# A long convolution beside block attention on one core: filter turned by TensorE, loads on one queue, a split last product, and a new instruction order

## The chip, the cores and the metric

The kernel runs on one NeuronCore of a Trainium2 chip. The core has five engines that run side by side and meet through semaphores: TensorE (PE, matmuls; its weight loads are listed as PEld), VectorE (DVE), ScalarE (ACT), GpSimd (POOL) and SyncE (SP, which here only issues DMAs). A DMA can be issued from SP, ACT or POOL; it takes its place in that engine's instruction stream. The metric is the device time of one execution in microseconds (us). The profile covers one execution; its span runs from the first to the last instruction, and the time lies a little above it.

## The reference

Two independent computations share the kernel, and their outputs stand side by side in the columns of the result.

```python
# A: gated long convolution, S = 2048 positions, D = 640 channels
k_shift = sum(k_pad[:, t:t+S, :] * shift_k[:, ks-1-t] for t in range(4))
kv = k_shift * v
y  = irfft(rfft(kv, 2*S) * rfft(ssm_k, 2*S))[:S] + kv * ssm_D
a  = q * y
# B: 32 heads of 20, four segments of 512 positions
for s in range(4):
    p     = softmax(q_s @ k_s^T * scale + causal_mask)
    a_mem = phi(q_s) @ M / (phi(q_s) @ z + 1e-6)
    o_s   = g * a_mem + (1 - g) * (p @ v_s)
    M, z  = M + phi(k_s)^T @ v_s, z + sum(phi(k_s))
b = concat(o) @ wo
out = concatenate([a, b], axis=-1)
```

## The kernel before, in words

**Part A** runs over five blocks `dp` of 128 channels (`a_chunks`). The transform is done as matmuls with the tables `Wf` (forward) and `Wi` (inverse) for each of four phases `c` (position = 4p + c), joined by butterflies on DVE. For each block: `load_kv` fetches `vt` (v) and `kr` (k, transposed by DMA); `kshift` makes the short filter on PE with the diagonal weights `skd`, and DVE multiplies into `vt`; `fwd("X", c)` transforms it, ACT casting each PSUM bank into `F`; `bfly("X")` is the DVE butterfly into `Xh`. The long filter takes the same way: `load_sk` fetches 128 rows of `ssm_k`, DVE copies them so that the phases stand together (`kT<-kT`, a COPY of 128x2048), a DMA transposes the copy into `kT`, and `fwd("K", c)` and `bfly("K")` give `Kh`. Then DVE multiplies the spectra into `S` (`pointwise`, `ybfly`), PE inverts (`inverse`), DVE multiplies with q into `outa`, and POOL stores it.

**Part B** runs over eight units `u`, that is four segments `s` and two halves of 16 heads. `b_proj_chunks` loads x transposed (`xT`), projects it with `wqkv` in four pieces of 128 positions (three groups of five matmuls each into the two `b` banks; ACT casts them to `KQ` and `Va`; DMAs transpose `KQ` into `KT` and `QT`), and finds a bound for each row of logits (`bound`: `kam`, `A`, `tq`, `bT`), which four small DMAs put into row 20 of each 32-row band of `QT`. `b_attn_chunks` spreads `KT` into `KZ` (POOL DMAs) and does four groups `attn(g)`: logits on PE into the three `st` banks, exp on ACT into `ET`, causal mask on DVE, product with `Va` and the memory into the one `o` bank, and division and sum on DVE into `o_s`. After the second half of a segment four DMAs transpose `o_s` into `oT` (`outt`), and `outproj` multiplies with `wo`: two groups of 320 columns for each of four pieces, cast by ACT into `outb`, stored by POOL.

**Order.** No order is written by hand. `Recorder` records all operations, prices each (`price`), and `plan` runs a list scheduler forwards and backwards with the priorities of the table `BIAS` and the earliest times of the table `HOLD`; `emit` then issues them in that order, so each engine's stream is fixed before the run. Every operation carries a key such as `('A', dp, stage)`. All emitted instructions therefore carry the line of `emit` (L435 before, L438 after). PSUM has eight banks: 3 `st`, 2 `a` (part A), 2 `b`, 1 `o`.

DMAs on the hardware queues (SP and ACT) get one of eight semaphores, `DMAHW0` to `DMAHW7`, in turn; a DMA waits at its issue until the one eight before it has landed. The listings of order show these waits.

Of the kernel before, what the change touches and what calls it, by code (L numbers as in the profile page):

```python
# [15 lines left out]
ALU = mybir.AluOpType  # L16
# [64 lines left out]
class Op:  # L81
    __slots__ = ("eng", "calls", "key", "bank", "new", "dur", "lat", "dma", "pred", "succ", "tail", "idx", "late")
# [11 lines left out]
class Recorder:  # L94


    def __init__(self, tc):
        self.tc, self.real = tc, tc.nc
        self.nc = ProxyNC(self)
        self.ops, self.key = [], ("const",)  # L100
        self.live, self.masks = {}, {}
        self.slots, self.home, self.turn, self.rows = {}, {}, {}, {}
# [32 lines left out]
    def add(self, eng, method, args, kw):  # L135
# [3 lines left out]
        e = QUEUES[eng]  # L139
# [6 lines left out]
        if method == "matmul" and bank.last is not None and bank.last.eng == "PE":  # L146
            op = bank.last
        if op is None:
# [3 lines left out]
            op.pred, op.succ, op.dur, op.lat = {}, [], 0.0, 0.0  # L152
            self.ops.append(op)
            if bank is not None:
                bank.left += 1
                bank.ops.append(op)
# [22 lines left out]
    def price(self, op, method, out, ins):  # L179
# [5 lines left out]
        elif method in ("dma_start", "dma_start_transpose"):  # L185
            src = ins[0]
            size = int(np.prod(list(out.shape))) * mybir.dt.size(out.dtype)
            if method == "dma_start_transpose":
                packets, per = size / 256, 23.5
                dram = src.space == bass.MemoryType.DRAM  # L190
                op.dur = 650.0 + 560.0 * size / 131072 + (600.0 if dram else 0.0)
# [6 lines left out]
        elif op.eng == "ACT":  # L198
            op.dur, op.lat = n / 1.152 + 33, 210.0
        elif op.eng == "DVE":  # L200
            fast = all(two(a) and a.space != bass.MemoryType.PSUM and int(a.ap[-1][0]) == 1 for a in [out] + ins)
            if method == "tensor_tensor":
                op.dur = n / (1.92 if fast else 0.96) + 60
            elif method == "tensor_reduce":
                op.dur = int(np.prod(list(ins[0].shape)[1:])) / 0.96 + 60
            elif method == "reciprocal":
                op.dur = 67 + 6.1 * n
            else:
                op.dur = n / (3.84 if fast else 1.2) + 60
# [65 lines left out]
    def backward(self, prio):  # L275
# [19 lines left out]
        while times:  # L295
# [3 lines left out]
            for e in free:  # L299
# [34 lines left out]
                for p in o.late:  # L334
                    j = p.idx
                    r = end + (0 if p.dma is None and p.eng == e and e != "PE" else self.lag(p))
# [8 lines left out]
    def forward(self, prio, held):  # L345
# [19 lines left out]
        while times:  # L365
# [3 lines left out]
            for e in free:  # L369
# [31 lines left out]
                else:  # L401
                    fin, near = end + o.lat, end + (0 if e != "PE" else o.lat)
# [41 lines left out]
class K3:  # L444
    def __init__(self, ctx, tc, A_q, A_k, A_v, A_shift_k, A_ssm_k, A_ssm_D, B_x, B_wq, B_wk, B_wv, B_wo, B_beta, out):
# [30 lines left out]
        def wload(engs, half):  # L476
# [67 lines left out]
    def a_chunks(self, dp):  # L544
# [6 lines left out]
        def load_sk():  # L551
            sk = self.ring("kT", [128, 4, 4, 128], n=2)[:].rearrange("p a b d -> p (a b d)")
            nc.sync.dma_start(out=sk, in_=self.ssm_k[dsl, :])
            skp = self.ring("kT", None, n=2)
            nc.vector.tensor_copy(out=skp[:], in_=sk.rearrange("d (b p c) -> d c b p", b=4, c=4))
            Drow = st["Drow"] = self.ring("Drow", [1, 128])
            nc.gpsimd.dma_start(out=Drow[:], in_=self.ssm_D[None, dsl])
            kT = st["kT"] = self.ring("kT", None, n=2)
# [114 lines left out]
        Kc = [(load_sk, 0.1)] + [(fwd("K", c), 2.0) for c in range(4)] + [(bfly("K"), 5.5)]  # L673
# [3 lines left out]
    def b_proj_chunks(self, u):  # L677
# [32 lines left out]
        def bound():  # L710
# [37 lines left out]
        return ch  # L748

    def b_attn_chunks(self, u):  # L750
# [13 lines left out]
        def attn(g):  # L764
            def f():
# [21 lines left out]
                for qh in range(2):  # L787
# [19 lines left out]
                    else:  # L807
                        o2 = self.ring("o2", [128, 2, 8, DH], n=2)
                        V.tensor_tensor(out=o2[:], in0=pov[:, :, :, 0:DH], in1=rr[:, :, :, None].to_broadcast([128, 2, 8, DH]), op=ALU.mult)
                        V.tensor_tensor(out=odst, in0=o2[:, 0].rearrange("p (q h) e -> p q h e", h=4), in1=o2[:, 1].rearrange("p (q h) e -> p q h e", h=4), op=ALU.add)  # L810
# [18 lines left out]

        ch = [(attn(g), 7.0) for g in range(4)]  # L830
        pre = [(spread(g), 0.1) for g in range(2)]
        tail = [(outt, 0.1)] + [(outproj(t), 1.5) for t in range(4)] if half == 1 else []
# [130 lines left out]
```

## Time and profile before

| | us |
|---|---|
| three runs | 355.88, 362.82, 357.06; median 357.06 |
| the profiled execution's own time | 355.69 |
| its span | 353.7 |
| PE busy / DVE busy / ACT busy / POOL busy | 302.4 / 305.7 / 278.0 / 80.5 |
| mean granted TensorE clock | 0.97 of full speed |

Three engines are each busy for more than three quarters of the span. The shares alone do not say which one holds the time, so the span is best cut into a start, a long middle and an end, with each engine's busy time in each piece. In the profile's rows, "idle before" names what ended an engine's idle time; in the chain of waits each row is a start, a duration, and what held the chain then. A row such as `SPq ... DMA_TRANSPOSE` gives the time in which SP was issuing, not the time in which the data moved. Names are `out<-in` with buffer numbers left out.

### The profile page before, as it was taken

How to read it: one execution, taken by the hardware profiler on the slowest of the kernel's cores; microseconds unless marked ns; L12 is line 12 of the kernel's file. 1: busy time of each engine (PE TensorE's matmuls, PEld its weight loads, DVE VectorE, ACT ScalarE, POOL GpSimd, SP SyncE). 2: the span in 40 equal slices, each digit the busy share in tenths (PEclk: the TensorE clock that was granted, in tenths of full speed). 3: DMA queues.
4: the chain of work that ended last, by engine and by line, in shares of the span. 5: the costliest groups of instructions: out<-in, count | busy, mean ns of one | idle time of the engine just before them, and what ended most of it. 6: DMA issues, size and time to landing. Idle time of an engine off the chain costs nothing.

```text
span 353.7 us, 9016 instructions
## 1 busy us (share of the span) xinstructions
PE 302.4 (86%) x3462; PEld 217.8 (62%) x3466; DVE 305.7 (86%) x539; ACT 278.0 (79%) x633; POOL 80.5 (23%) x127
## 2 busy tenths in 40 slices
PE   0179699899997699799999999999989998888584
PEld 0157477567785477577766776777766675555363
DVE  2016999999999999899999999999998998999960
ACT  1046648999979989889989999989986998899502
POOL 9402410214112110312024005230060040312023
PEclk9999999999999899899999999999998999999869
DMA  9976766969557335705598358537430564302043
GB/s 262 212 141 165 159 141 98 256 117 199 112 114 186 73 62 113 134 17 74 150 130 202 74 126 142 117 68 105 100 92 26 91 105 70 92 30 69 0 101 110
DMA packets 110267, 40.97 MB, mean 116 GB/s; under 512 B 102624, under 2 KB 107264, under 8 KB 109968
## 3 DMA queue, kind: packets, MB, share of 16 engines
q1 hardware_dynamic: 100768, 29.50, 43.7%
q0 software_dynamic: 5088, 8.09, 8.9%
q10 hardware_dynamic: 4368, 2.81, 2.8%
q8 instruction: 27, 0.44, 0.5%
q14 instruction: 16, 0.13, 0.1%
HBM read 13.36 MB, written 5.24 MB: 53 GB/s over the span
## 4 chain that ended last, share of the span: by engine, by line
PE 33%; DVE 28%; issue 14%; DMA 8%; ACT 6%; SPq 6%; POOL 3%; POOLq 0%; ACTq 0%; DVEq 0%
PE b L435 13%; PE a L435 9%; PE st L435 7%; DVE S L435 7%; SPq L435 6%; PE o L435 4%; DVE ET L435 4%; DMA KT<-KQ 3%; DVE Xh L435 3%; ACT ET L435 3%; DVE kam L435 3%; DMA kr<-in_A_k_dram 2%; POOL out_dram L435 2%; DMA oT<-o_s 1%; DVE o L435 1%
## 5 line engine op out<-in xcount | busy, mean ns | idle before, releaser
L435 ACT ACTIVATE ET<-st 128x512 bf16<-128x512 f32 (+1 forms) x384 | 185.2, 575 | 11.6 <-PE st L435 10.5
L435 PE MATMUL st<-QT,KZ 128*128 128x384 bf16 (+2 forms) x508 | 105.1, 301 | 6.3 <-ACT ET L435 3.9
L435 PE MATMUL b<-wqkv,xT 128*128 128x320 bf16 x480 | 79.3, 303 | 18.8 <-DMA xT<-in_B_x_dram 16.0
L435 PEld LDWEIGHTS <-xT 128*128 128x128 bf16 x480 | 45.8, 99 | 37.6 <-DMA xT<-in_B_x_dram 16.0
L435 POOL DMA_DIRECT2D KZ<-KT x64 | 40.0, 629 | 123.0 <-PE st L435 91.1
L435 PEld LDWEIGHTS <-KZ 128*128 128x128 bf16 x512 | 45.6, 98 | 28.0 <-issue 12.2
L435 PEld LDWEIGHTS <-ET 128*128 128x128 bf16 x1280 | 41.8, 96 | 24.1 <-DVE ET L435 11.5
L435 PE MATMUL o<-Va,ET 128*128 128x21 bf16 x1280 | 44.2, 173 | 12.0 <-DVE ET L435 5.9
L435 ACT CAST F<-a 128x512 bf16<-128x512 f32 x80 | 48.4, 624 | 5.5 <-PE a L435 5.0
L435 ACT CAST KQ<-b 128x320 bf16<-128x320 f32 x64 | 30.0, 472 | 19.4 <-PE b L435 17.4
L435 DVE TENSOR_TENSOR ET<-ET,cmask 128x1024 bf16<-128x1024 bf16 x64 | 43.0, 682 | 0.4 <-ACT ET L435 0.4
L435 PEld LDWEIGHTS <-Wf 128*128 128x128 bf16 x320 | 30.3, 99 | 15.8 <-issue 8.8
L435 DVE TENSOR_TENSOR S<-S 128x2048 bf16<-128x2048 bf16 (+1 forms) x40 | 37.2, 950 | 0.2
L435 POOL DMA_DIRECT2D out_dram<-outa x20 | 15.4, 769 | 71.5 <-DVE outa L435 52.7
L435 PE MATMUL b<-wo,oT 128*128 128x320 bf16 x160 | 28.0, 314 | 0.6 <-DMA oT<-o_s 0.6
L435 PE MATMUL a<-kT,Wf 128*128 128x256 bf16 x160 | 24.3, 274 | 2.9 <-DVE outa L435 1.9
L435 ACT CAST outb<-b 128x320 bf16<-128x320 f32 x32 | 14.9, 480 | 14.1 <-PE b L435 14.1
L435 DVE TENSOR_TENSOR o<-o,rr 128x320 bf16<-128x320 f32 x48 | 23.6, 491 | 1.6
L435 PE MATMUL a<-vt,Wf 128*128 128x256 bf16 x160 | 23.3, 280 | 1.4 <-ACT F L435 0.7
L435 PE MATMUL a<-S,Wi 128*128 128x256 bf16 x160 | 22.2, 286 | 1.5 <-DVE S L435 1.5
L435 DVE TENSOR_TENSOR S<-Xh,Kh 128x4096 bf16<-128x4096 bf16 x10 | 22.8, 2284 | 0.1
L435 PE MATMUL a<-skd,kr 128*128 128x128 bf16 x320 | 22.0, 224 | 0.4 <-DMA kr<-in_A_k_dram 0.2
(61 smaller groups left out, 385.0 us busy)
## 6 DMA issues: line engine op xcount, KB each, us to landing
KZ<-KT POOLq DMA_DIRECT2D x64, 42.0 KB, 2.9
kT<-in_A_ssm_k_dram SPq DMA_DIRECT2D x5, 512.0 KB
qd<-in_A_q_dram SPq DMA_DIRECT2D x20, 128.0 KB
out_dram<-outa POOLq DMA_DIRECT2D x20, 128.0 KB, 2.8
out_dram<-outb POOLq DMA_DIRECT2D x16, 160.0 KB, 2.1
vt<-in_A_v_dram SPq DMA_DIRECT2D x16, 128.0 KB
Wf<-c_wf ACTq DMA_DIRECT2D x1, 1024.0 KB
Wi<-c_wi SPq DMA_DIRECT2D x1, 1024.0 KB
```

The costliest lines, as they stand in the source:

```text
L435: f(*[fix(a) for a in args], **{k: fix(v) for k, v in kw.items()})
```

## The change

1. **Long filter.** The DVE copy and the DMA transpose of `load_sk` are gone. A new stage `turn(c)`, four for each block, multiplies four strided slices of the loaded rows with the identity on PE (128x128 each, into one `a` bank), and ACT casts the bank into `kT`. The loaded rows now have a buffer `sk` of their own, one, and `kT` is one buffer instead of two.
2. **Loads.** `Wf`, the first half of the projection weights (three loads) and the four `vt` loads of block 0 are issued on SP instead of ACT. `skc`, `ident`, `kr` and `xT` were on SP already.
3. **Bound rows.** The four DMAs from `bT` into `QT` become one with a partition step of 32.
4. **Last product.** For the last segment `o_s` is kept as features 0 to 511 and features 512 to 639. Four DMAs transpose the first part, one the second. The product with `wo` is made 512 columns wide in four banks (three `st`, one `b`) over the first four feature blocks, and the last feature block is added later, in a separate piece; the remaining 128 columns go to one `b` bank. DVE and ACT share the casts, and SP and ACT issue the stores. Head group 3 of the last unit lies in the second part alone.
5. **Planner.** Prices change (a stall of 115 ns after a reciprocal, ACT on SBUF data dearer, DVE copies from PSUM cheaper), and `BIAS` and `HOLD` are replaced whole, so the order changes everywhere.

```diff
         def load_sk():
-            sk = self.ring("kT", [128, 4, 4, 128], n=2)[:].rearrange("p a b d -> p (a b d)")
-            nc.sync.dma_start(out=sk, in_=self.ssm_k[dsl, :])
-            skp = self.ring("kT", None, n=2)
-            nc.vector.tensor_copy(out=skp[:], in_=sk.rearrange("d (b p c) -> d c b p", b=4, c=4))
+            sk = st["sk"] = self.ring("sk", [128, S])
+            nc.sync.dma_start(out=sk[:], in_=self.ssm_k[dsl, :])
+            st["kT"] = self.ring("kT", [128, 4, 4, 128])
...
-            nc.sync.dma_start_transpose(out=kT[:].rearrange("p c b d -> p (c b) d"), in_=skp[:].rearrange("d c b p -> d (c b p)"))
+        def turn(c):
+            def f():
+                ps = self.bank("a")
+                phase = st["sk"][:].rearrange("d (b p c) -> d c b p", b=4, c=4)
+                for b in range(4):
+                    nc.tensor.matmul(ps[:, 128 * b:128 * b + 128], lhsT=phase[:, c, b, :], rhs=ident[:], start=True, stop=True)
+                nc.scalar.copy(out=st["kT"][:, c], in_=ps[:].rearrange("p (b d) -> p b d", d=128))
+            return f
...
-            "Wf": lambda: nc.scalar.dma_start(out=self.Wf[:], in_=self.real.inline_tensor(Wf_np, name="c_wf").ap()),
+            "Wf": lambda: nc.sync.dma_start(out=self.Wf[:], in_=self.real.inline_tensor(Wf_np, name="c_wf").ap()),
-            "w0": wload((nc.scalar,) * 3, 0), "w1": wload((nc.sync,) * 3, 1),
+            "w0": wload((nc.sync,) * 3, 0), "w1": wload((nc.sync,) * 3, 1),
-                (nc.scalar if dp == 0 else nc.sync).dma_start(out=vt[:, b], in_=self.v[512 * b:512 * b + 512, dsl].rearrange("(p c) d -> p c d", c=4))
+                nc.sync.dma_start(out=vt[:, b], in_=self.v[512 * b:512 * b + 512, dsl].rearrange("(p c) d -> p c d", c=4))
...
-            for hl in range(4):
-                r = 32 * hl + DH
-                nc.sync.dma_start(out=QT[r:r + 1, :, :], in_=bT[4 * hl:4 * hl + 4, :])
+            nc.sync.dma_start(out=QT[DH:128:32, :, :], in_=bT[:])
...
+        def out_last():
+            oT = self.ring("oT", None)
+            low, high = self.o_parts(s)
+            for tci in range(4):
+                nc.sync.dma_start_transpose(out=oT[:, 0:4, 128 * tci:128 * tci + 128], in_=low[:, tci, :])
+            nc.sync.dma_start_transpose(out=oT[:, 4, :].rearrange("p (t k) -> p t k", t=4), in_=high)
+            wide = [self.bank(k) for k in ("st", "st", "st", "b")]
+            edge = self.bank("b")
+            for ccs in (range(4), (4,)):
+                for tci in range(4):
+                    self.rec.cut = ccs[0] == 4
...
+            fin = self.ring("ET", None, n=2)[:, :, 0:640]
+            for tci in range(4):
+                (nc.scalar.copy if tci % 2 else V.tensor_copy)(out=fin[:, tci, 0:512], in_=wide[tci][:])
...
+                (nc.scalar if tci % 2 else nc.sync).dma_start(out=self.out[L * s + 128 * tci:L * s + 128 * tci + 128, D:2 * D], in_=fin[:, tci, :])
...
 BIAS = {
-    ('A', 0, 0): 5055, ('A', 0, 1): 3361, ('A', 0, 10): 288761, ('A', 0, 11): 15357, ('A', 0, 12): 174774, ('A', 0, 13): 17992, ('A', 0, 14): -17162,
...
+    ('A', 0, 0): 89953, ('A', 0, 1): 438151, ('A', 0, 10): 1950, ('A', 0, 11): 160004, ('A', 0, 12): -11423, ('A', 0, 13): 619533, ('A', 0, 14): 147551,
```

Three places show how the order moved. The first is SP at the start of the program. Before, with the waits in brackets:

```order
L435 DMA kT_99<-in_A_ssm_k_dram 128x2048
L435 DMA_TRANSPOSE xT_113<-in_B_x_dram 128x5x512
L435 DMA skc<-in_A_shift_k_dram 128x5x4
L435 DMA ident<-c_ident 128x128
L435 DMA_TRANSPOSE kT_99<-kT_100 128x16x128 [waits DMAHW1_49,DMAHW0_49,DVE_49]
L435 DMA_TRANSPOSE kr_105<-in_A_k_dram 128x512
```

SP in the changed kernel at the same place, without the waits; `sk_99` is what was loaded into `kT_99`:

```order
L438 DMA Wf<-c_wf 128x4096
L438 DMA ident<-c_ident 128x128
L438 DMA sk_99<-in_A_ssm_k_dram 128x2048
L438 DMA skc<-in_A_shift_k_dram 128x5x4
L438 DMA_TRANSPOSE xT_113<-in_B_x_dram 128x5x512
L438 DMA wqkv<-in_B_wk_dram 128x5x320
L438 DMA wqkv<-in_B_wq_dram 128x5x320
L438 DMA wqkv<-in_B_wv_dram 128x5x320
L438 DMA_TRANSPOSE kr_105<-in_A_k_dram 128x512 x3
L438 DMA vt_104<-in_A_v_dram 128x4x128
L438 DMA_TRANSPOSE kr_105<-in_A_k_dram 128x512
L438 DMA vt_104<-in_A_v_dram 128x4x128 x3
```

The tables and the filter now stand ahead of `xT`, and one queue holds every large load in one row.

The second place is ACT at the start, before, where it issues loads between its casts (`KQ`, `Va` and `xm` belong to the projection):

```order
L435 DMA Wf<-c_wf 128x4096
L435 DMA vt_104<-in_A_v_dram 128x4x128 [waits DMAHW2_49]
L435 ACT_TABLE_LOAD
L435 CAST KQ_80<-b_66 128x16x20 [waits PE_49]
L435 ACTIVATE xm_115<-KQ_80 128x320 [waits Activation_49]
L435 DMA vt_104<-in_A_v_dram 128x4x128 [waits DMAHW7_49]
L435 CAST KQ_80<-b_67 128x16x20 [waits PE_49]
L435 DMA bt<-in_B_beta_dram 128x32 [waits DMAHW0_49]
L435 CAST Va_83<-b_66 128x16x20 [waits PE_49]
```

ACT at the start of the changed kernel:

```order
L438 ACT_TABLE_LOAD
L438 CAST kT_100<-a_64 128x512 [waits PE_49]
L438 CAST kT_100<-a_65 128x512 [waits PE_49]
L438 CAST kT_100<-a_64 128x512 [waits PE_49]
L438 CAST F_102<-a_65 128x512 [waits PE_49]
L438 CAST F_102<-a_64 128x512 [waits PE_49]
L438 CAST F_102<-a_65 128x512 [waits PE_49]
L438 CAST F_102<-a_64 128x512 [waits PE_49]
L438 CAST kT_100<-a_65 128x512 [waits PE_49]
L438 CAST F_102<-a_64 128x512 [waits PE_49]
L438 CAST F_102<-a_65 128x512 [waits PE_49]
L438 CAST KQ_80<-b_66 128x16x20 [waits PE_49]
```

The filter's casts now come first and the projection's after them; only `bt` is still loaded from ACT here.

The third place is DVE at the end of the program, before (`o_128` and `o_129` are the two buffers `o2`, `outa` the gated output of part A):

```order
L435 TENSOR_TENSOR outa_112<-a_64,qd_108 128x512
L435 RECIPROCAL rr_124<-o_68 128x16
L435 TENSOR_TENSOR o_129<-o_68,rr_124 128x320
L435 TENSOR_TENSOR o_s_120<-o_129 128x2x80
L435 TENSOR_TENSOR outa_111<-a_65,qd_108 128x512
L435 TENSOR_TENSOR outa_112<-a_64,qd_108 128x512
```

DVE at the end of the changed kernel:

```order
L438 TENSOR_TENSOR outa_112<-a_64,qd_108 128x512
L438 TENSOR_TENSOR o_128<-o_68,rr_123 128x320
L438 TENSOR_TENSOR o_s_120<-o_128 128x2x80
L438 RECIPROCAL rr_124<-o_68 128x16
L438 TENSOR_TENSOR o_129<-o_68,rr_124 128x320
L438 TENSOR_TENSOR o_s_120<-o_129 128x2x80
L438 CAST ET_121<-b_66 128x128 x2
L438 CAST ET_121<-st_62 128x512
L438 CAST ET_121<-st_61 128x512
```

All of part A's outputs now stand ahead of the last `o_s`, and behind it are only the casts of the last product. On PE, 8 of the 20 wide matmuls now stand ahead of the last group's second product with `Va` and 8 right behind it; the 20 of 128 columns and the other 4 wide ones come last.

More of the change, by code (lines that the diff above doesn't have):

```diff
@@ L81 @@
 class Op:
-    __slots__ = ("eng", "calls", "key", "bank", "new", "dur", "lat", "dma", "pred", "succ", "tail", "idx", "late")
+    __slots__ = ("eng", "calls", "key", "bank", "new", "dur", "lat", "dma", "pred", "succ", "tail", "idx", "late", "stall")
 class Bank:
@@ L100, in __init__ @@
         self.ops, self.key = [], ("const",)
-        self.live, self.masks = {}, {}
+        self.live, self.masks, self.cut = {}, {}, False
         self.slots, self.home, self.turn, self.rows = {}, {}, {}, {}
@@ L145, in add @@
         op = None
-        if method == "matmul" and bank.last is not None and bank.last.eng == "PE":
+        if method == "matmul" and bank.last is not None and bank.last.eng == "PE" and not self.cut:
             op = bank.last
+        self.cut = False
         if op is None:
@@ L151, in add @@
             op.new = bank is not None and bank.last is None
-            op.pred, op.succ, op.dur, op.lat = {}, [], 0.0, 0.0
+            op.pred, op.succ, op.dur, op.lat, op.stall = {}, [], 0.0, 0.0, 0
             self.ops.append(op)
             if bank is not None:
+                if not op.new:
+                    op.pred[bank.ops[0].idx] = bank.ops[0]
                 bank.left += 1
@@ L189, in price @@
                 packets, per = size / 256, 23.5
-                dram = src.space == bass.MemoryType.DRAM
-                op.dur = 650.0 + 560.0 * size / 131072 + (600.0 if dram else 0.0)
+                op.dur = 650.0 + 570.0 * size / 131072
             else:
@@ L198, in price @@
         elif op.eng == "ACT":
-            op.dur, op.lat = n / 1.152 + 33, 210.0
+            op.dur, op.lat = n / 1.152 + (33 if ins[0].space == bass.MemoryType.PSUM or n > 1000 else 95), 210.0
         elif op.eng == "DVE":
+            op.stall = 115 if method == "reciprocal" else 0
             fast = all(two(a) and a.space != bass.MemoryType.PSUM and int(a.ap[-1][0]) == 1 for a in [out] + ins)
@@ L208, in price @@
             else:
-                op.dur = n / (3.84 if fast else 1.2) + 60
+                op.dur = n / (3.84 if fast else 1.9) + 60
             op.lat = 150.0
@@ L335, in backward @@
                     j = p.idx
-                    r = end + (0 if p.dma is None and p.eng == e and e != "PE" else self.lag(p))
+                    r = end + (p.stall if p.dma is None and p.eng == e and e != "PE" else self.lag(p))
                     ready[j] = max(ready[j], r)
@@ L401, in forward @@
                 else:
-                    fin, near = end + o.lat, end + (0 if e != "PE" else o.lat)
+                    fin, near = end + o.lat, end + (o.stall if e != "PE" else o.lat)
                 done_at[i] = fin
@@ L672, in a_chunks @@
         X = [(load_kv, 0.1)] + [(kshift(a), 1.5) for a in range(4)] + [(fwd("X", c), 2.0) for c in range(4)] + [(bfly("X"), 7.0)]
-        Kc = [(load_sk, 0.1)] + [(fwd("K", c), 2.0) for c in range(4)] + [(bfly("K"), 5.5)]
+        Kc = [(load_sk, 0.1)] + [(turn(c), 1.0) for c in range(4)] + [(fwd("K", c), 2.0) for c in range(4)] + [(bfly("K"), 5.5)]
         Dl = [(load_q, 0.1), (pointwise(0), 4.6), (pointwise(1), 5.0), (ybfly, 7.6)] + [(inverse(c), 1.7) for c in range(4)]
@@ L748, in b_proj_chunks, with o_parts, o_pieces @@
         return ch
+    def o_parts(self, s):
+        o = self.o_s[s][:].rearrange("p t h d -> p (t h d)")
+        return o[:, 0:2048].rearrange("p (t f) -> p t f", t=4), o[:, 2048:2560].rearrange("p (t f) -> p t f", t=4)
+    def o_pieces(self, s, f0, q0):
+        if s < NS - 1:
+            return [(self.o_s[s][:].rearrange("p t h d -> p t (h d)")[:, q0:q0 + 2, f0:f0 + 80], 0, 80)]
+        low, high = self.o_parts(s)
+        cut = min(max(512 - f0, 0), 80)
+        return ([(low[:, q0:q0 + 2, f0:f0 + cut], 0, cut)] if cut else []) + ([(high[:, q0:q0 + 2, f0 + cut - 512:f0 + 80 - 512], cut, 80)] if cut < 80 else [])
     def b_attn_chunks(self, u):
@@ L809, in f @@
                         V.tensor_tensor(out=o2[:], in0=pov[:, :, :, 0:DH], in1=rr[:, :, :, None].to_broadcast([128, 2, 8, DH]), op=ALU.mult)
-                        V.tensor_tensor(out=odst, in0=o2[:, 0].rearrange("p (q h) e -> p q h e", h=4), in1=o2[:, 1].rearrange("p (q h) e -> p q h e", h=4), op=ALU.add)
+                        loc, mem = (o2[:, x].rearrange("p (q h) e -> p q (h e)", h=4) for x in range(2))
+                        for dst, a, b in self.o_pieces(s, h0 * DH, 2 * qh):
+                            V.tensor_tensor(out=dst, in0=loc[:, :, a:b], in1=mem[:, :, a:b], op=ALU.add)
             return f
@@ L828, in outproj @@
             return f
+        def out_last():
+            oT = self.ring("oT", None)
+            low, high = self.o_parts(s)
+            for tci in range(4):
[6 more added lines that the diff above has]
+                    self.rec.cut = ccs[0] == 4
+                    for cc in ccs:
+                        nc.tensor.matmul(wide[tci][:], lhsT=oT[:, cc, 128 * tci:128 * tci + 128], rhs=self.wo[:, cc, 0:512], start=(cc == 0), stop=(cc == 4))
+            for tci in range(4):
+                for cc in range(5):
+                    nc.tensor.matmul(edge[:, 128 * tci:128 * tci + 128], lhsT=oT[:, cc, 128 * tci:128 * tci + 128], rhs=self.wo[:, cc, 512:640], start=(cc == 0), stop=(cc == 4))
+            fin = self.ring("ET", None, n=2)[:, :, 0:640]
+            for tci in range(4):
+                (nc.scalar.copy if tci % 2 else V.tensor_copy)(out=fin[:, tci, 0:512], in_=wide[tci][:])
+                (V.tensor_copy if tci % 2 else nc.scalar.copy)(out=fin[:, tci, 512:640], in_=edge[:, 128 * tci:128 * tci + 128])
+                (nc.scalar if tci % 2 else nc.sync).dma_start(out=self.out[L * s + 128 * tci:L * s + 128 * tci + 128, D:2 * D], in_=fin[:, tci, :])
         ch = [(attn(g), 7.0) for g in range(4)]
         pre = [(spread(g), 0.1) for g in range(2)]
-        tail = [(outt, 0.1)] + [(outproj(t), 1.5) for t in range(4)] if half == 1 else []
+        tail = [] if half == 0 else [(out_last, 0.1)] if s == NS - 1 else [(outt, 0.1)] + [(outproj(t), 1.5) for t in range(4)]
         return pre, ch, tail
@@ L837 @@
 BIAS = {
[34 rows of a table removed]
-    ('beta',): -57426, ('const',): 401682, ('load', 'Wf'): -285064, ('load', 'Wi'): -16407, ('load', 'w0'): 90126, ('load', 'w1'): -10388,
-    ('load', 'wo'): -34008,
[38 rows of a table added]
 }
 HOLD = {
[9 rows of a table removed]
[8 rows of a table added]
 }
```

1 line of the change is left out of this document (removed), and 87 rows, old and new, of tables (BIAS, HOLD).

## The prediction

> **What bounds the kernel now.** I read the busy times by stage first, then the chain of waits at the start, then the end. The first view's columns are the stretch, its length, busy time (and count) of PE, PEld, DVE, ACT and POOL, granted clock, DMA share and GB/s. I cut at three DVE events: its first long run (30.58), the first butterfly of X (43.79), and the end of the last `o_s` (341.47 + 0.24 = 341.71).
>
> ```profile
> 0.00:30.58 30.58, 12.29 (x84) 8.13 (x85) 4.82 (x11) 9.35 (x20) 13.97 (x20) 1.00 0.91 203
> 30.58:43.79 13.21, 10.05 (x110) 7.99 (x107) 12.96 (x21) 7.34 (x16) 4.09 (x7) 1.00 0.64 149
> 43.79:341.71 297.92, 272.70 (x3221) 196.56 (x3226) 286.57 (x506) 257.94 (x590) 58.77 (x95) 0.97 0.53 105
> 341.71:353.70 11.99, 7.40 (x52) 5.14 (x50) 1.39 (x3) 3.41 (x8) 3.71 (x6) 0.93 0.42 116
> ...
> 240.00:260.00 20.00, 19.89 (x265) 15.10 (x263) 19.79 (x35) 19.03 (x46) 2.15 (x4) 1.00 0.52 95
> ...
> 30.58 1.23 DVE L435 TENSOR_TENSOR Kh<-F 128x2048 bf16<-128x2048 bf16 x1 [0.15 <-ACT F L435]
> ...
> 43.79 1.22 DVE L435 TENSOR_TENSOR Xh<-F 128x2048 bf16<-128x2048 bf16 x1
> ...
> 341.47 0.24 DVE L435 TENSOR_TENSOR o_s<-o 128x160 bf16<-128x160 bf16 x1
> ```
>
> From 30.58 to 341.71 DVE idles 0.25 + 11.35 us in 311: it carries the kernel there. In the third stage PE idles 25.2 and ACT 40.0. DVE's other idle time is 25.8 us at the start and 10.6 at the end. So span = X butterfly's start + DVE's work from there to the last `o_s` + its idle + tail.
>
> The start: the chain of waits (start, duration, holder) and who waited for `xT`:
>
> ```profile
> 1.21 7.91 SPq L435
> ...
> 18.01 4.15 DMA kr<-in_A_k_dram
> 22.16 0.02 issue
> 22.18 0.56 ACTq L435
> 22.74 0.04 issue
> 22.78 0.43 ACT KQ L435
> ...
> 24.77 0.45 PE a L435 x4
> ...
> PE b L435 <- DMA xT<-in_B_x_dram: 16.0, 1, 16.0
> ```
>
> PE does nothing until `xT` lands at 16.0; its issue takes 7.91 us while four large loads from ACT share the DMA engines. Later a `vt` load on ACT waits for a `kr` transfer until 22.18, and the casts queue behind it.
>
> **The change: the start.** What PE needs first is now `Wf`, `ident` and `sk`.
>
> ```profile
> 2.00:4.00 2.00, 0.00 (x0) 0.00 (x0) 0.00 (x0) 0.00 (x0) 2.00 (x1) 1.00 0.90 296
> ...
> kT<-in_A_ssm_k_dram SPq DMA_DIRECT2D x5, 512.0 KB
> ...
> Wf<-c_wf ACTq DMA_DIRECT2D x1, 1024.0 KB
> ...
> L435 SPq DMA_TRANSPOSE xT<-in_B_x_dram x4: 2899/4466/7912, 1.2 to 216.3; - x4
> ...
> 16.70 5.17 SPq L435 DMA_TRANSPOSE kr<-in_A_k_dram  x4
> ...
> 59.38 1.73 SPq L435 DMA_DIRECT2D Wi<-c_wi  x1
> ...
> 24.14 0.55 ACTq L435 DMA_DIRECT2D vt<-in_A_v_dram  x1
> ...
> L435 ACT CAST F<-a 128x512 bf16<-128x512 f32 x80 | 48.4, 624 | 5.5 <-PE a L435 5.0
> ...
> L435 ACT ACTIVATE xm<-KQ 128x320 bf16<-128x320 bf16 x24 | 12.1, 505 | 1.9 <-DVE PK L435 0.9 <-DVE Mbd L435 0.7
> ...
> 29.44 0.18 DVE L435 TENSOR_SCALAR omginv<-ep 128x32 f32<-128x32 f32 x1 [7.27 <-ACT ep L435]
> ```
>
> 1.5 MB at the 296 GB/s of 2:4 are 5 us after 2.0: the turns start near 7. In its new order ACT then makes 4 `kT` and 8 `F` casts at 0.6 (7.2 us), six projection casts at the chain's 0.43 (2.6), two `xm` and one load, some 0.5 each (1.5): 11.3 us, so the last `F` comes at 18.5, provided `xT` is there when its first cast is due, near 13. Behind the 1.5 MB, with its median issue of 4.47, `xT` should land at about 12. So DVE's long run starts at 18.5 instead of 30.58. Up to the X butterfly it has its 12.96 us, less the 1.22 of the copy (below), plus the 1.1 of `beta` work that it had done from 29.44 to 30.58: 31.4, if it never waits. It also needs `vt`. SP's issues are `Wf` 1.7 (as `Wi`), `xT` 2.9 to 7.9, `kr` 5.2, ten more at 0.55 and 0.8 of gaps: the last `vt` is issued by 17 to 22, against 24.69. After it come the short filter, four forward phases and `kam`, which I let cost DVE 2 us of waits: X butterfly at 33.5 (31.4 to 37), a gain of 10.3. The stall of ACT's loads moves to SP; behind SP's loads stand only loads and the first `KT` and `QT`, whose casts are not made before 14 to 16.
>
> A rule speaks against this. The Trainium skill, Perfetto Trace Analysis, DMA Optimizations, advises balancing DMAs over the engines that can issue them when issuing is the bottleneck. By it, with `xT` at its longest, the last `vt` comes 3 us earlier instead of about 6 and the sum is some 3 us longer; the trace has no start from one queue to decide it, but it shows ACT's casts held by a load.
>
> **The middle.** `kT` alone in the second and third stage (PE, DVE, clock, DMA share, GB/s), a run of 32 matmuls of 128x128, the `o_s` additions (min/median/max ns), and two rows on the bound:
>
> ```profile
> 30.58:43.79 13.21, 0.00 (x0) 1.22 (x1) 1.00 0.64 149
> 43.79:341.71 297.92, 19.70 (x128) 3.94 (x3) 0.97 0.53 105
> ...
> 30.05 1.95 PE a L435 x32
> ...
> L435 DVE TENSOR_TENSOR o_s<-o x48: 178/233/244, 140.9 to 341.5; 128x160 bf16<-128x160 bf16 x48
> ...
> 45.88 2.07 SPq L435 DMA_DIRECT2D QT<-bT  x3
> ...
> PE st L435 <- DMA QT<-bT: 1.2, 1, 1.2
> ```
>
> DVE: 286.57, less three copies (3.94), plus the two `outa` that stood behind the last `o_s` (the fourth stage's 1.39), plus two extra `o_s` pieces (0.4): 284.4. The copies' removal is worth its full price, since DVE is the bound.
>
> PE: 80 turn matmuls at 1.95 / 32 = 0.061, 60 of them in the middle: 3.7. Their weights are read with a step of four elements, which no row shows; bounds are 0.061 and the 0.45 / 4 = 0.11 of the chain's transform matmuls of double width, and I take 0.061, the row of the same size. The Trainium skill, VectorE: DVE Perf Modes, The three transpose paths, gives TensorE 390 ns for one 128x128; by that the 60 would be 23.4 us instead of 3.7 (an estimate), and PE would have more work than DVE. The run of 32 at 0.061 decides for the small price.
>
> ACT: 20 casts at 0.624, 15 in the middle: 9.4 on 257.94. It still idles 30 us, so I cost them at nothing; the cover is DVE's queue of work. If ACT's order delayed exps, PE's products and DVE's masks would be late next.
>
> SP: five transposes and 24 small DMAs fewer. The bound row comes up to three issues of 0.69 sooner, but PE waited for it once, for 1.2 us: between 0 and 1.2 gained, or a little lost if one DMA with 16 rows lands later than four small ones; I take 0. The single `sk` buffer makes the next filter's load wait for the turns, with `KT` and `QT` transposes behind it on SP; the turns run well ahead of those casts in the order, so 0, at worst a few us of the idle below.
>
> DVE's idle, 11.35, I set to 13: PE and ACT are fuller. The row 240:260 has all three above 19 of 20 us with DVE idle 0.21, 3 us over the whole middle; 25, PE's own idle, is the other end.
>
> **The tail.** From the last `o_s` to the end was 11.99.
>
> ```profile
> 140.67 3.13 DMA KT<-KQ
> ...
> 288.75 5.04 DMA oT<-o_s
> ...
> 32.00 0.68 PE b L435 x5
> ...
> 349.92 0.55 POOL L435 DMA_DIRECT2D out_dram<-outb  x1 [0.86 <-ACT outb L435]
> ```
>
> Now: one transpose, 3.1 to 5.0 from issue to user (3.9); 20 matmuls of 128 at 0.061 and 4 of 512 at 0.68 / 5 x 512 / 320 = 0.22 (2.1); casts after the last matmul 0.7; a second store's issue 0.6; store to end 3.8 (353.7 - 349.92), plus hand-overs 0.4: 11.5 (10.5 to 13). The wide product's head start saves 3.5 us of PE at a place where four 320-wide pairs already ran behind transposes, so little is won.
>
> **Sum.** 33.5 + 284.4 + 13 + 11.5 = 342.4 of span, plus 355.69 - 353.7 = 2.0: 344.4 us. That is against the profiled execution's own 355.69 (-3.2%); the median of the runs shown, 357.06, is 1.4 above that.
>
> **Rivals.**
> - *PE becomes the bound.* PE's middle is 272.70 + 3.7 + two inverse groups 2.1 + 16 wide matmuls 3.5 = 282. If it keeps its 25.2 idle, the middle is 307.2 and the time 354.2. For it: PE's 94% of 297. Against: the row 240:260, PE 19.89 of 20. This rival also holds the case that turns do not pipeline.
> - *The start brings nothing but the copy.* If one queue delivers `xT` and `vt` no sooner, the X butterfly comes at 43.79 - 1.22 = 42.6 and the time is 353.5. For it: 0.91 DMA share before 30.58. Against: 12 us in which PE could turn and transform, and ACT freed of loads.
> - *Slower: the clock.* If a fuller PE is granted less, PE binds.
>
> ```profile
> 146.00:148.00 2.00, 0.14 (x6) 0.14 (x6) 1.97 (x4) 2.00 (x4) 1.91 (x4) 1.00 1.27 225
> 148.00:150.00 2.00, 2.00 (x43) 2.00 (x41) 1.90 (x4) 1.30 (x3) 0.78 (x1) 0.62 0.89 146
> ...
> 320.00:340.00 20.00, 14.20 (x195) 9.18 (x195) 18.95 (x37) 11.49 (x28) 2.79 (x4) 0.82 0.16 38
> ```
>
> At 0.82 throughout the middle, 282 x 0.97 / 0.82 = 333.6 and the time is 380.6. Slower by 2% (364.2) begins at a middle of 317.2, a mean clock of 0.86. Against: the clock fell after PE had idled (0.14 of 2 us), and was 1.00 at 19.89 of 20.
>
> **Chances and range.** Forecast 0.70, PE 0.13, start 0.11, clock 0.06. Two per cent, 349.9 to 364.2, is about what a measurement of this kernel tells from no change (its three runs span 1.9%). The first two rivals end within 2%; milder forms of them, some 0.04, lie below 349.9: faster 0.74, same 0.20, slower 0.06. The forecast's own range is 338 (butterfly at 31.4, idle 9, tail 11) to 350 (idle 17, butterfly at 35); up to 354 it takes in most of both rivals.
>
> **What would show it.** Right: `Kh<-F` at 17 to 20 and the first `Xh<-F` at 31 to 37; DVE busy 284 to 285 from there to the last `o_s`, idle 9 to 17; kT casts on ACT at 0.6 with turn matmuls at 0.06; a tail of 10.5 to 13. Wrong: the butterfly later than 40, DVE idle over 20 with PE never idle, or a mean clock below 0.9.

## The result and the profile after

The changed kernel takes 339.53 us (median of four runs, 338.22 to 343.19), the kernel before, run beside it, 358.79 (355.88 to 362.82): a ratio of 0.951 (95% interval 0.938 to 0.963). Times are medians of all runs of a kernel, while ratios compare means without its slow runs (here without the 362.82), so a ratio isn't the quotient of two medians. The profiled execution took 339.53 us, with a span of 337.3. The forecast was 344.4, with a range of 338 to 354.

The same four stages as in the prediction, after, cut at the first `Kh<-F`, the first `Xh<-F` and the end of the last `o_s` (columns: stretch, length, busy time and count of PE, PEld, DVE, ACT, POOL, granted clock, DMA share, GB/s):

```profile
0.00:19.47 19.47, 11.27 (x76) 7.92 (x77) 1.83 (x6) 10.37 (x19) 11.13 (x17) 1.00 0.86 225
19.47:35.50 16.03, 13.20 (x140) 10.67 (x139) 13.23 (x26) 9.62 (x22) 5.48 (x11) 1.00 0.81 171
35.50:327.78 292.28, 275.59 (x3304) 201.69 (x3303) 278.14 (x507) 262.21 (x604) 60.76 (x97) 0.98 0.53 104
327.78:337.30 9.52, 3.19 (x28) 1.82 (x28) 1.78 (x5) 1.51 (x4) 0.00 (x0) 0.99 0.27 83
```

The span lost 16.4 us: 8.3 before X's butterfly, 5.6 in the middle, 2.5 at the end. DVE idles 2.8 us in the second stage and 14.1 in the third. The chain that ended last lies on PE for 60% of the span and on DVE for 9% (before: PE 33%, DVE 28%); the experiments say how far that may be believed:

```profile
PE 60%; ACT 15%; DMA 12%; DVE 9%; issue 4%; SPq 0%; DVEq 0%; ACTq 0%
```

DVE's rows of the timeline after (start, duration, idle before and what ended it) show what came ahead of X's butterfly:

```profile
19.47 1.23 DVE L438 TENSOR_TENSOR Kh<-F 128x2048 bf16<-128x2048 bf16 x1 [0.19 <-ACT F L438]
...
31.69 2.29 DVE L438 TENSOR_REDUCE kam<-KT 128x4 f32<-128x2048 bf16 x1 [1.81 <-DMA KT<-KQ]
...
34.76 0.82 DVE L438 TENSOR_SCALAR tq<-QT 128x2048 int16<-128x2048 int16 x1 [0.52 <-DMA QT<-KQ]
35.50 1.20 DVE L438 TENSOR_TENSOR Xh<-F 128x2048 bf16<-128x2048 bf16 x1
```

Of the 2.8 us of waits, 2.3 are for the transposes of `KT` and `QT`. And the end, after, on all engines:

```profile
327.54 0.24 DVE L438 TENSOR_TENSOR o_s<-o 128x160 bf16<-128x160 bf16 x1
...
330.31 1.07 PE L438 MATMUL b<-wo,oT 128*128 128x128 bf16 x16 [1.11 <-DMA oT<-o_s]
...
331.64 0.59 PE L438 MATMUL st<-wo,oT 128*128 128x512 bf16 x2
...
333.05 0.60 ACT L438 CAST ET<-b 128x512 bf16<-128x512 f32 x1
333.20 0.84 ACTq L438 DMA_DIRECT2D out_dram<-ET  x2
```

From the end of the last `o_s` (327.78) it is 2.5 us to the products of the last transpose, 1.9 to the end of the matmuls (332.23), 1.4 to the last cast's end (333.65), and 3.65 to the end: 9.5.

### The profile page after: what moved, and what is told of

Its sections match the earlier page's. It is cut to its first block, busy times and chain, and to the rows that moved or that the text cites. A ratio compares the mean times of both kernels' runs of the same rounds, so it can differ in the third digit from the quotient of the medians.

```text
span 337.3 us, 9126 instructions
## 1 busy us (share of the span) xinstructions
PE 303.2 (90%) x3546; PEld 222.1 (66%) x3546; DVE 295.0 (87%) x540; ACT 283.7 (84%) x649; POOL 77.4 (23%) x123
## 4 chain that ended last, share of the span: by engine, by line
PE 60%; ACT 15%; DMA 12%; DVE 9%; issue 4%; SPq 0%; DVEq 0%; ACTq 0%
PE b L438 20%; PE a L438 17%; PE st L438 15%; ACT ET L438 10%; PE o L438 7%; DMA QT<-KQ 6%; DMA kr<-in_A_k_dram 2%; ACT F L438 2%; DMA sk<-in_A_ssm_k_dram 2%; DVE S L438 2%; DVE tq L438 2%; DMA oT<-o_s 1%; DVE ET L438 1%; DVE o L438 1%; ACT KQ L438 1%
## 5 line engine op out<-in xcount | busy, mean ns | idle before, releaser
L438 ACT ACTIVATE ET<-st 128x512 bf16<-128x512 f32 (+1 forms) x384 | 193.4, 642 | 6.8 <-PE st L438 6.1
L438 PE MATMUL st<-QT,KZ 128*128 128x512 bf16 (+3 forms) x512 | 109.4, 303 | 6.1 <-ACT ET L438 5.2
L438 ACT CAST F<-a 128x512 bf16<-128x512 f32 x80 | 51.7, 674 | 2.8 <-PE a L438 2.7
L438 ACT CAST KQ<-b 128x320 bf16<-128x320 f32 x64 | 33.7, 526 | 6.9 <-PE b L438 4.0
L438 PE MATMUL a<-kT,Wf 128*128 128x256 bf16 x160 | 26.0, 289 | 0.7 <-ACT F L438 0.6
L438 PE MATMUL b<-wo,oT 128*128 128x320 bf16 (+2 forms) x145 | 23.2, 291 | 1.1 <-DMA oT<-o_s 1.1
L438 PE MATMUL a<-skd,kr 128*128 128x128 bf16 x320 | 21.1, 219 | 1.3 <-DMA kr<-in_A_k_dram 1.1
L438 DVE TENSOR_REDUCE kam<-KT 128x4 f32<-128x2048 bf16 x8 | 18.2, 2275 | 4.0 <-DMA KT<-KQ 4.0
L438 PEld LDWEIGHTS <-kr 128*128 128x128 bf16 x320 | 19.3, 98 | 3.1 <-issue 1.7
```

The costliest lines, as they stand in the source:

```text
L438: f(*[fix(a) for a in args], **{k: fix(v) for k, v in kw.items()})
```

## Experiments

The runs keep the order of the kernel that they alter, except where the edit moves something: it is made after planning. Ratios are to the kernel before, run beside them. The third stage ("middle") of each profiled execution, cut as above:

| | time, us | ratio (95%) | middle | DVE busy | DVE idle | PE busy |
|---|---|---|---|---|---|---|
| before | 358.79 | 1 | 297.92 | 286.57 | 11.35 | 272.70 |
| after | 339.53 | 0.951 (0.938 to 0.963) | 292.28 | 278.14 | 14.14 | 275.59 |
| after_again | 342.32 | 0.953 (0.946 to 0.961) | 295.90 | 278.49 | 17.41 | 277.68 |
| pair | 346.30 | 0.964 (0.954 to 0.974) | 301.67 | 286.48 | 15.19 | 281.44 |
| more | 344.39 | 0.960 (0.951 to 0.968) | 298.16 | 275.78 | 22.38 | 278.52 |
| split (of before) | 358.34 | 0.996 (0.990 to 1.001) | 296.45 | 281.42 | 15.03 | 269.62 |
| dve_more | 358.57 | 1.004 (0.998 to 1.010) | 311.22 | 300.10 | 11.12 | 278.94 |
| act_more | 343.95 | 0.964 (0.956 to 0.972) | 296.37 | 278.48 | 17.89 | 274.76 |
| pe_more | 343.10 | 0.961 (0.954 to 0.969) | 293.97 | 278.46 | 15.51 | 278.79 |
| old_tail | 346.91 | 0.971 (0.962 to 0.980) | 292.79 | 277.15 | 15.64 | 273.44 |
| act_loads | 340.22 | 0.947 (0.942 to 0.952) | 295.31 | 278.05 | 17.26 | 274.90 |
| dma_turn | 347.16 | 0.967 (0.962 to 0.973) | 295.84 | 282.65 | 13.19 | 273.22 |
| rows4 | 344.76 | 0.961 (0.955 to 0.966) | 295.84 | 278.02 | 17.82 | 273.72 |
| conv_split | 341.99 | 0.953 (0.949 to 0.958) | 297.71 | 278.91 | 18.80 | 275.96 |

**after_again.**

> The changed kernel unaltered, as the measure for the kernels beside it: span 337 to 340, and in the middle DVE 278 busy and 14 idle, as in the execution shown.

DVE's work is the same to 0.35 us, the middle 3.6 us longer. So one profile tells a change of the middle only beyond some 4 us; DVE's busy time is far steadier. The last section shows where most of the 3.6 went.

**Why is DVE's work in the middle 6.3 us below the forecast?** DVE's timeline before, at one reciprocal and its reader:

```profile
107.11 0.20 DVE L435 RECIPROCAL rr<-o 128x8 f32<-128x8 f32 x1
107.34 0.32 DVE L435 TENSOR_TENSOR o_s<-o,rr 128x160 bf16<-128x160 f32 x1
```

The reader starts 0.03 us after the reciprocal's end. After, at the like place:

```profile
101.48 0.20 DVE L438 RECIPROCAL rr<-o 128x8 f32<-128x8 f32 x1
101.60 0.65 DVE L438 TENSOR_TENSOR outa<-a,qd 128x512 bf16<-128x512 f32 x1
102.16 0.32 DVE L438 TENSOR_TENSOR o_s<-o,rr 128x160 bf16<-128x160 f32 x1
```

Another product stands between, and starts 0.08 before the reciprocal's end. Over all rows of DVE's two timelines the medians are the same: a reader starts 0.03 to 0.04 after the end of what it reads, any other instruction 0.08 before the end of the one ahead. In the stream before, 60 of 64 reciprocals stand right ahead of their reader, in the stream after 3. The planner's prices now hold a stall after a reciprocal. To undo that alone, each reciprocal is moved:

```diff
+        if o.calls[0][1] == "reciprocal":
+            wait[next(q for q in o.succ if q.eng == "DVE").idx] = o
+            continue
+        if o.idx in wait:
+            out.append(wait.pop(o.idx))
         out.append(o)
```

*pair.*

> Changed kernel; each of the 64 reciprocals is moved to just ahead of its reader on DVE, all else stays in its order. Theory (neighbours): an instruction on DVE that reads what the one right before it wrote starts 0.03 us after that one's end, any other 0.08 before it, so each dependent pair costs 0.11 us. Dependent reciprocals go from 3 to 64: 61 x 0.11 = 6.7 us more of DVE in the middle, and 5 to 7 us more of span if DVE carries the middle. Rival 1 (DVE got shorter by shorter instructions or by work moved to other stages): less than 1 us. Rival 2 (PE now sets the end, as 60% of the chain suggests): DVE's time grows by 6 us but the span by 0 to 2.

DVE's busy time goes from 278.3 (the mean of the two unaltered runs) to 286.48, and the middle to 301.67, 5.8 to 9.4 us longer. The edit makes 61 dependent pairs with reciprocals and nine others (neighbours in DVE's stream of which the second reads the tile that the first wrote): 8.2 / 70 = 0.117 us each. Rival 1 falls. Rival 2 falls by the middle, which grew beyond the 4 us between runs; part of that growth may be PE's, since its granted clock was 0.96 here and 0.97 to 0.98 in the unaltered runs. The ratios (0.964 against 0.951 and 0.953) point the same way with overlapping intervals, and *dve_more* below tests it harder. The same place in its timeline, and its middle:

```profile
101.33 0.20 DVE L438 RECIPROCAL rr<-o 128x8 f32<-128x8 f32 x1
101.56 0.32 DVE L438 TENSOR_TENSOR o_s<-o,rr 128x160 bf16<-128x160 f32 x1
```

```profile
35.02:336.69 301.67, 281.44 (x3304) 203.84 (x3303) 286.48 (x507) 263.69 (x604) 60.56 (x97) 0.96 0.52 101
```

The reader starts 0.03 us behind the reciprocal again.

*split* and *more* go the other way: the reader of a result, where it stands right behind it, changes places with the instruction behind it, in the kernel before (reciprocals alone) and in the changed one (all).

```diff
+        between = order[j + 1:k + 1]
...
+        order[j:k + 1] = between + [b]
```

> Kernel before; 41 of its 60 reciprocals that stand right ahead of their readers get another instruction between (the reader changes places with the one behind it). Neighbours: 41 x 0.11 = 4.5 us less of DVE in the middle (286.6 busy to about 283, idle less by 1 too) and 3 to 4.5 us less of span. Rival 1: less than 1 us of difference.

> Changed kernel; of the DVE instructions that still follow the one whose result they read, 41 change places with the instruction behind them. Neighbours: 41 x 0.11 = 4.5 us less of DVE; the span falls by 2 to 4.5 if DVE carries it. Rival 1: no change. Rival 2 (PE sets the end): 0 to 1 less, or a little more, since 41 results come one instruction later.

In *split* DVE's work falls by 5.1, as the theory says, but the middle by 1.5 only, which is less than runs differ by, and the time not measurably: its interval allows a gain of 3.6 us (1%) at most. In *more* DVE's work falls by 2.5, and its idle time grows by 5 to 8. That is 0.126 and 0.06 us for each swap; *more* took every kind of dependence, not only a result that is read. So the price holds, but taking pairs out by a blind swap doesn't pay: DVE's idle time grew where its work fell, and that the later results are waited for is the likely reason, not a shown one.

**Which engine carries the middle?** Work was added to each of the three, with the values left as they are.

```diff
+        if o.key[0] == "A" and o.calls[0][1] == "tensor_tensor" and tuple(o.calls[0][3]["out"].shape)[1:] == (2, 8, 2, 128):
+            o.calls = o.calls * 2
```

> Changed kernel; the five large products S<-Xh,Kh of pointwise(0), i = 0, are made twice on DVE (same values). 5 x 2.2 = 11 us more of DVE in the middle (278 to 289). Theory (balance: DVE, PE and ACT are all near full, so work added to any of them lengthens the middle by most of its price, while work taken away brings little): 8 to 11 us of span. Rival (PE alone sets the end now): 0 to 3.

```diff
+        if o.eng == "ACT" and o.calls[0][1] == "copy" and o.calls[0][3]["out"].tensor.name.startswith("kT"):
+            o.calls = o.calls * 2
```

> Changed kernel; the 20 kT casts on ACT are made twice. 20 x 0.55 to 0.63 = 11 to 12.6 us more of ACT, 16 of them in the middle (262 to about 271). My prediction costed kT casts at nothing in the middle: 0 to 2 us of span beside 1 to 2 at the start. Balance theory: 5 to 10 us.

```diff
+        if o.calls[0][1] == "matmul" and o.calls[0][3]["lhsT"].tensor.name.startswith("sk0"):
+            o.calls = o.calls * 3
```

> Changed kernel; the 80 turn matmuls are made three times. 160 more at 0.061 are 9.8 us of PE, at 0.11 17.6; three quarters of it in the middle: the growth of PE's busy time prices one. If PE alone sets the end: the middle grows by all of it, 7 to 13 us. If DVE does: 0 to 3. Balance: 4 to 10.

*dve_more* doubled the products of both halves i, ten and not five, so DVE got 21.8 us more, not 11. The middle grew by 15.3 to 18.9 of them:

```profile
34.66:345.88 311.22, 278.94 (x3304) 202.38 (x3303) 300.10 (x517) 263.61 (x604) 60.29 (x97) 0.97 0.47 98
```

That is 0.70 to 0.87 for each us of DVE; the time grew by some 18 (against 340.8, the median of the eight unaltered runs). *act_more* put 8 us more on ACT in the middle and *pe_more* 1 to 3 on PE; the middles (296.37 and 293.97) lie within 0.5 us of the unaltered ones, and the times are 2 to 3 us up, of which 0.5 to 1.7 stand in the start (X's butterfly at 35.95 and 36.60). The granted clock of both middles was 0.99, against 0.98 and 0.97, so a small price of the added work may be hidden in them. So DVE does carry the middle, and the chain's 60% of PE isn't the price of PE's work: a chain follows the last releaser, and where three engines are nearly full it passes through all of them. *pe_more* also prices one turn matmul by the groups of both kernels. After:

```profile
L438 PE MATMUL a<-ident,sk 128*128 128x128 bf16 x80 | 8.8, 247 | 7.9 <-DMA sk<-in_A_ssm_k_dram 7.5 <-ACT kT L438 0.2
```

pe_more:

```profile
L438 PE MATMUL a<-ident,sk 128*128 128x128 bf16 x240 | 18.7, 238 | 8.2 <-DMA sk<-in_A_ssm_k_dram 8.1
```

160 more cost 9.9 us, 0.062 each. The mean of 238 to 247 ns in the same rows is the length of one in the pipeline, not its price.

**The start: queue or turn?** In *act_loads* the loads are on ACT again:

```diff
+        if o.key in (("load", "Wf"), ("load", "w0")) or o.dma is not None and o.eng == "SP" and o.calls[0][3]["out"].tensor.name.startswith("vt0") and o.key[1] == 0:
+            o.calls = [("scalar", m, a, kw) for _, m, a, kw in o.calls]
```

> Changed kernel; Wf, the first halves of the projection weights and block 0's four vt loads are issued from ACT again (as before), in the same order. My prediction: ACT's first casts are held behind issues and behind a vt load that waits, so the first Kh<-F comes 1 to 4 us later than 19.2 and X's butterfly 2 to 6 later than 35. Rival (the skill's balancing rule, as weighed in the prediction): two issuing queues bring xT and vt about 3 us sooner, and the butterfly is at 32 to 34.

The first `Kh<-F` came at 19.71, against 19.16 and 19.47, and X's butterfly at 33.97, against 34.86 and 35.50. So the single queue costs X's butterfly 0.9 to 1.5 us; in the time (340.22 against 340.8) no difference can be told. SP's issue of the first `KT` transpose, after:

```profile
18.74 1.23 SPq L438 DMA_TRANSPOSE KT<-KQ  x1
```

and in act_loads, with DVE's first user:

```profile
15.34 1.21 SPq L438 DMA_TRANSPOSE KT<-KQ  x1
...
29.97 2.28 DVE L438 TENSOR_REDUCE kam<-KT 128x4 f32<-128x2048 bf16 x1
```

SP reaches it 3.4 us sooner without those loads ahead of it, and `kam` no longer waits 1.81. ACT's casts weren't held in this order, so the stall that the prediction saw in the trace of before isn't a matter of the queue alone. The Trainium skill (Perfetto Trace Analysis, DMA Optimizations) advises sharing DMAs out over the engines that can issue them where issuing is the bottleneck. The run agrees in sign, with about 1 us where the prediction had weighed 3.

*dma_turn* undoes the turn:

```diff
+                o.calls = [("vector", "tensor_copy", [], dict(out=Y.rearrange("d (c b p) -> d c b p", c=4, b=4), in_=X.rearrange("d (b p c) -> d c b p", b=4, c=4))),
+                           ("sync", "dma_start_transpose", [], dict(out=X.rearrange("p (k d) -> p k d", d=128), in_=Y))]
```

> Changed kernel; the turn is undone: no turn matmuls and kT casts, instead one DVE copy and one DMA transpose for each block, at the place of its first turn, in the same order otherwise. Prediction's terms: DVE 5 x 1.22 us more, of which four in the middle (+5); in the start Kh<-F 3 to 6 us later, since copy, issue and transfer stand between sk and the first transform. Together 8 to 14 us. PE also waits in its order for four later transposes (about 5 us each); if those waits aren't covered, more than 14. Rival (the turn is worth only its copies): 4 to 6.

`Kh<-F` came at 25.69 and X's butterfly at 39.95: 4.5 to 5.1 us later, within what was expected of the start. Of this some 1.5 us can be the copy's own delay: it took 3.68 beside a POOL memset, where the first copy of the kernel before took 2.17. The POOL memset, its DVE copy beside that, and the first transform:

```profile
6.28 3.52 POOL L438 MEMSET KZ<- 128x4096 bf16 x1
...
7.20 3.68 DVE L438 COPY kT<-sk 128x2048 bf16<-128x2048 bf16 x1 [7.20 <-DMA sk<-in_A_ssm_k_dram]
...
15.38 3.57 PE L438 MATMUL a<-sk,Wf 128*128 128x256 bf16 x16 [15.38 <-DMA sk<-kT]
```

In the middle DVE has 4.3 us more, yet the middle (295.84) is no longer than in unaltered runs: the copies' own price isn't seen above the 4 us between runs. In all the time is some 6 us longer, less than the 8 to 14 expected: 4.5 to 5.1 of it stand in the start and 1.8 at the end (11.31). There the granted clock was 0.73, and PE's 28 matmuls took 4.67 us for 3.19, so most of the 1.8 isn't the turn's own price.

**rows4.**

> Changed kernel; each bound row is carried by four DMAs again. Prediction: 0 to 1.2 us. Rival (24 more issues of 0.6 to 0.7 on SP delay KT and QT transposes behind them): DVE and PE idle more in the middle, 2 to 5 us.

```diff
+            o.calls = [("sync", "dma_start", [], dict(out=dst[hl:hl + 1], in_=src[4 * hl:4 * hl + 4])) for hl in range(4)]
```

All four stages of its profiled execution lie within 0.3 us of after_again's, but its times (342.67 to 346.41) lie some 4 us above the unaltered median, with overlapping intervals. Whether the single transfer is worth 0 or some 4 us stays open.

**old_tail.**

> Changed kernel with the former end: o_s in its former layout (one addition per group), four transposes, the product in 320-wide halves on two banks, casts on ACT alone, stores from POOL; all else in its order. If the form of the end is worth what the two traces differ by, the time from the last o_s to the end goes from 9.5 back to 12.0 us. If the gain came from the emptier queues and engines around it, 9.5 to 10.5.

```diff
+        put.append(("sync", "dma_start_transpose", [], dict(out=oT[:, :, 128 * tci:128 * tci + 128], in_=o_s[:, tci, :, :])))
...
+        put.append(("gpsimd", "dma_start", [], dict(out=K.out[L * s + 128 * tci:L * s + 128 * tci + 128, D:2 * D], in_=outb[tci % 2][:].rearrange("p a b -> p (a b)"))))
```

In this layout and order two additions overwrite columns 0 to 159 of the third segment's last 128 rows before their transpose, so values there change; the work doesn't. The end takes 14.87 us, more than either theory:

```profile
325.87 0.24 DVE L438 TENSOR_TENSOR o_s<-o 128x160 bf16<-128x160 bf16 x1
326.18 5.20 SPq L438 DMA_TRANSPOSE oT<-o_s  x4
327.69 0.24 DVE L438 TENSOR_TENSOR o_s<-o 128x160 bf16<-128x160 bf16 x1
...
339.03 0.54 POOL L438 DMA_DIRECT2D out_dram<-outb  x1 [2.20 <-ACT outb L438]
```

The last two additions stand 1.8 us apart in this order. Before, they stood 5.1 apart, the second at 341.47:

```profile
336.32 0.24 DVE L435 TENSOR_TENSOR o_s<-o 128x160 bf16<-128x160 bf16 x1
336.63 7.67 SPq L435 DMA_TRANSPOSE oT<-o_s  x4
```

So there the first two transposes lay ahead of the end, and here they don't. The new form is worth 5.3 us in the new order.

**conv_split**, an attempt at a better version.

> Changed kernel; 12 long-convolution instructions on DVE that follow the one they read change places with a short one behind them, and four of the five skd products move from DVE to POOL. 12 x 0.11 + 4 x 0.6 = 3.7 us less of DVE. If DVE carries the middle: 2 to 4 us less than the changed kernel. If the middle is balanced, or a KZ transfer behind a skd on POOL comes late: 0, or up to 2 more.

```diff
+    split(rec, lambda o: o.key[0] == "A")
...
+            o.calls = [("gpsimd", m, a, kw) for _, m, a, kw in o.calls]
```

DVE's work did not fall at all (278.91), and the time isn't better. A DVE instruction and the POOL product beside it:

```profile
74.74 2.32 DVE L438 TENSOR_TENSOR Xh<-Xh 128x1024 bf16<-128x1024 bf16 x1
...
75.44 1.05 POOL L438 TENSOR_TENSOR skd<-ident,skc 128x512 bf16<-128x512 bf16 x1
```

The butterfly step, 0.68 elsewhere, took 2.32. Beside the other three products a step of 0.68 took 1.53, an `xm` of 0.23 took 1.08 and a mask of 0.68 took 1.37. Together that is 4.0 us, about what the four moved products (0.69 each) and the 12 swaps should have saved: what DVE was spared it lost to POOL.

No run here was measurably faster than the changed kernel (act_loads, 0.947, has an interval that takes in its 0.951).

## Why the prediction was right, and where not

The span was 337.3 for 342.4. By the terms of the sum, the start came out 2.0 longer, DVE's work 6.3 shorter, DVE's idle time 1.1 longer and the tail 2.0 shorter. That start and tail cancel is luck; what is left is DVE's work, less a little by the idle time.

- **Bound.** Right: DVE carries the middle (*dve_more*, *pair*), PE and ACT had room for the turns (*act_more*, *pe_more*). "The copies' removal is worth its full price, since DVE is the bound" went too far: added work was paid at 0.7 to 1.1, but work taken away at 0.3 in the profile of *split* (0 to 0.7 by its times) and not at all in *more*. Whether that is because PE and ACT follow closely, or because the swapped results come later, no run tells. With the copies put back (*dma_turn*, which also takes the turns from PE and ACT) the middle stayed within what unaltered runs differ by.
- **Start, 33.5 against 35.5** (34.9 in the second run). Right in its parts: turns at 7.52, `Kh<-F` at 19.47 for 18.5, 2.8 us of waits for 2. Of the 8.3 us gained, the turn is worth 4.5 to 5.1 in the new order, though some 1.5 of that can be the copy held by POOL. Wrong that one queue helps: it costs X's butterfly 0.9 to 1.5. What is left, some 4 to 5 us, is probably the new order's; no run took it apart. The start before isn't fixed either: in *split*, whose start is unaltered, X's butterfly came at 45.42 and not 43.79.
- **DVE's work, 284.4 against 278.1.** This is the mis-sized term. The prediction counted instructions added and removed and left out their neighbours. 57 reciprocal pairs fewer at 0.117 are 6.7 us, which gives 277.7. But other dependent pairs became more: in DVE's timelines of the middle, rows that don't overlap the one ahead go from 109 to 62, only 47 fewer, since there are ten more of other kinds (`o_s<-o` right behind its `o`, for one, from 12 to 18). 47 at 0.117 are 5.5 of the 6.3; the rest stays open. The row for it, a reciprocal with its reader 0.03 behind, was in the trace of before, and the stall of 115 ns in the diff.
- **DVE's idle, 13 against 14.1.** Right within what runs differ by; the second run's 17.4 lies just above the 9 to 17 that were named.
- **kT casts on ACT at nothing, turn matmuls at 0.061.** Right: 8 us more of casts in the middle can't be told from none, and a turn matmul costs 0.062. By the Trainium skill's 390 ns for one (VectorE: DVE Perf Modes, The three transpose paths) the 160 extra ones would have cost 62 us (an estimate); they cost 9.9.
- **Tail, 11.5 against 9.5.** Transpose to user 2.5 for 3.9, matmuls 1.9 for 2.1, casts 1.4 for 0.7, then 3.65 for 4.8 of store and hand-overs. "So little is won", on the wide product, was wrong for the new order, where the former end would have taken 14.9.
- **Bound rows at 0.** Open.
- **Clock.** No loss: 0.98 in the middle, but it makes part of the difference between runs (below).

## What to carry to other kernels

Price neighbours, not only instructions: a dependent DVE pair cost 0.117 us, and over the 57 reciprocals moved off their readers that is 6.7 us, more than the three copies (3.94) that the change took from the middle. Test a bound from both sides: work added to DVE was paid at 0.7 or more, work taken away at much less, for a reason that the runs leave open. A share of the chain that ended last isn't a price; adding work to that engine gives one.

## What the runs showed of the hardware

**POOL holds DVE.** Beside one memset a DVE copy took 3.68 us (1.22 in the prediction's rows), and beside a POOL product of 1.05 a butterfly step took 2.32 for 0.68. The Trainium skill (SBUF — State Buffer, SBUF: two separate sides) says that DVE, in some modes or with two inputs from SBUF, and GpSimd share a pair of ports under an exclusive lock, for the whole instruction. The rows agree: the copy ended 1.08 us after the memset's end (9.80), and the three steps beside POOL products that take 0.68 alone ended 0.54 to 0.57 us after the product's end. Why the one shown lost 1.64, more than the product's 1.05, stays open; POOL was issuing a DMA just before it.

**The clock after a pause.** In the changed kernel PE idles from 109 to 112 us, and then has half its clock for some 3:

```profile
109.00:110.00 1.00, 0.00 (x0) 0.00 (x0) 0.04 (x1) 0.09 (x1) 1.00 (x2) 1.00 1.36 204
...
111.00:112.00 1.00, 0.00 (x0) 0.00 (x0) 1.00 (x2) 1.00 (x2) 0.00 (x0) 0.89 1.30 205
112.00:113.00 1.00, 0.85 (x29) 0.85 (x29) 1.00 (x2) 1.00 (x4) 0.00 (x0) 0.50 0.68 86
...
115.00:116.00 1.00, 1.00 (x7) 0.34 (x6) 1.00 (x3) 0.62 (x3) 0.00 (x0) 0.90 0.00 0
116.00:117.00 1.00, 1.00 (x21) 0.92 (x20) 0.96 (x2) 0.61 (x2) 0.00 (x0) 1.00 0.00 0
```

Such pauses differ from run to run. From 40 to 60 us the changed kernel's first run kept its clock:

```profile
40.00:60.00 20.00, 18.93 (x212) 14.57 (x211) 19.27 (x29) 16.26 (x41) 0.14 (x1) 1.00 0.95 167
...
44.71 1.00 PE L438 MATMUL a<-skd,kr 128*128 128x128 bf16 x15 [1.07 <-DMA kr<-in_A_k_dram]
```

and after_again did not, with 2.6 us less of DVE's work done, most of the 3.6 by which its middle is longer:

```profile
40.00:60.00 20.00, 17.83 (x187) 13.73 (x186) 16.71 (x25) 13.94 (x34) 0.14 (x1) 0.91 0.87 143
...
45.19 1.00 PE L438 MATMUL a<-skd,kr 128*128 128x128 bf16 x15 [2.17 <-DMA kr<-in_A_k_dram]
```

The clock isn't the first cause there. PE had waited 2.17 us for a transfer, and not 1.07, and DVE's next product waited 1.30 for PE, and not 0.20: 1.1 of the 2.6 is the late transfer itself. The rest came after the clock had fallen to half from 47 to 49; that the fall cost it is likely, not shown.
